# The spectrum's columns in two halves, input blocks contiguous over 128 lanes, and the tables and folds of the prologue in another order

## The chip, the cores and the metric

One core of a Trainium2 chip runs the kernel. The metric is the time of one execution on the device in microseconds (us), as a median over runs. The engines are TensorE (PE; its weight loads are PEld), VectorE (DVE), ScalarE (ACT) and GpSimd (POOL); SP (SyncE) issues nearly all DMA transfers, from one queue in program order, and waits there for whatever a transfer needs.

## The reference

```python
L = 2 * S                                   # x: (8, 6336, 128), h: (6336, 128)
Yf = np.fft.rfft(x, n=L, axis=1) * np.fft.rfft(h, n=L, axis=0)[None]
y = np.fft.irfft(Yf, n=L, axis=1)[:, :S, :]          # causal convolution along the sequence
scores = np.einsum('bsd,d->bs', y, w_gate)
# per batch: the 128 rows with the highest score
out[b, top] = y[b, top] + sigmoid(scores[b, top]) * (relu(y[b, top] @ w1) @ w2)
```

All arrays are float32. A long convolution of eight batches is followed by an expert that changes 128 rows of each batch.

## The kernel before

The transform is done by matmuls in four stages: with 6400 = 50 x 128, **a** transforms over 50 points, **b** over 128 points and multiplies by the spectrum of h, **c** and **d** go back. The work is cut into eight units (four pairs of batches times two halves of the 128 channels). A unit has eight input blocks of x.

- `load_x` loads a block (one transfer of SP); `place` says where it waits: in `half` (the tile into which c writes), in one of three tiles `xr`, or in the spectrum itself. `fold` makes sums and differences of the block, two operations on VectorE or POOL (L104, L105). A block has 114 lanes of data, of which 100 are used.
- `stage_a(unit, q, t)` transforms half of block q (L136) and copies the result from PSUM into the spectrum `reg[unit % 2]` (L146 on VectorE, L148 on ACT).
- `stage_b(unit, c)` takes four of the 50 columns k: matmuls with a table `wt` (L163), two products with the h spectrum `ht` on VectorE (L184), two additions on POOL into `reg` (L190). There are 13 per unit. `load_b` loads `wt` and `ht` for it.
- `stage_c(unit, a)` takes four of 64 columns j out of `reg` (L201) and copies them into `half` (L202). There are 16 per unit.
- `stage_d(unit, i)` makes the output (L218, then L221 to L223), POOL multiplies by the gate (L226, tile `tm`), VectorE reduces it (L230), and SP stores it. There are eight per unit; `load_d` loads its tables.
- The search for the highest scores and the experts run as a *strand* after every second unit: after each piece of other work `visit` issues a little of it.

`plan` writes the order out by hand. The prologue is a of h, a of unit 0, then "j" (b of h and b of unit 0 for the same columns, with the h spectrum stored to `hd` in between) and a of unit 1. Then for each unit u: c of u in pairs alternating with b of u+1 in pairs, and a of u+2 alternating with d of u. While c of u empties `reg[u % 2]`, blocks of unit u+2 are loaded into the columns that c has read; `AREAS` is the order in which c reads. b's tables come from six buffers and are asked for two b ahead. PSUM has three tiles `pt`, used in turn; the tiles that `wide` gives are five buffers.

The reads of `stage_c` and the place of a block in the spectrum are these lines:

```python
w = yv[:, r, c * 4 + j, :, t]               # yv: p (r j k t); c * 4 + j is one of 64 columns j
v4 = reg[u % 2].rearrange("p (c z) -> p c z", c=4)[0:LN, :, (q + 3) * 400:(q + 4) * 400]
return v4[:, :, 0:256], v4[:, :, 256:384]   # the block in four pieces, one in each quarter
```

## Time and profile before

| | |
|---|---|
| median of 3 runs | 1182.99 us (1181.5 to 1185.68) |
| profiled execution | 1172.5 us, span 1170.7 us |
| PE busy / PEld busy | 844.7 us (72%) / 743.8 us (64%) |
| DVE / POOL / ACT busy | 661.7 us (57%) / 555.7 us (47%) / 464.9 us (40%) |
| transfers | 147.03 MB, mean 126 GB/s; SP's queue takes 39.9% of the DMA engines' time |
| mean granted clock of TensorE | 0.870 |

Busy time is an average over stages with different limits, so the stages have to be looked at one by one. A granted clock of 1.00 is 2.4 GHz, 0.50 is 1.2 GHz.

### The profile page before, as it was taken

Reading aid. Unit: us, or ns where it says so; the run is one execution under the profiler, and the core shown is the slowest. Engines: PE = TensorE matmul, PEld = TensorE weight load, DVE = VectorE, ACT = ScalarE, POOL = GpSimd, SP = SyncE. Lnnn points to the kernel's source line nnn. Section 1 sums busy time; section 2 is a strip of 40 time slices with the busy share of each in tenths; the row PEclk is TensorE's granted clock in tenths of the full one; section 3 lists DMA queues with packets and bytes.
Section 4 is the critical chain, followed back from the end, with each engine's and each line's share of the span. In section 5 each row is a group of like instructions: output and inputs, shape, how many; then the busy total and the mean of one; then the engine's idle time right before and its main releaser. Section 6 shows DMA issues by size and latency. Waiting matters only on the chain. (4 is left out here: it accounts for less than half of the span.)

```text
span 1170.7 us, 36897 instructions
## 1 busy us (share of the span) xinstructions
PE 844.7 (72%) x16143; PEld 743.8 (64%) x16143; DVE 661.7 (57%) x1008; ACT 464.9 (40%) x1179; POOL 555.7 (47%) x392
## 2 busy tenths in 40 slices
PE   6849787786778687785778686785678998677303
PEld 5737676675667566774667565774677877676303
DVE  2228544453544567675585456575574786516773
ACT  3413331251125433762344333663343365572241
POOL 3427735653645545544555545344554565304402
PEclk9669898997889989997899988998898998888756
DMA  4345344355434643354335444355425443503300
GB/s 154 159 166 189 112 138 108 114 187 152 115 104 129 184 134 118 107 172 143 107 115 157 137 114 125 98 160 159 122 85 163 147 124 116 173 2 118 105 0 10
DMA packets 87149, 147.03 MB, mean 126 GB/s; under 512 B 6866, under 2 KB 42264, under 8 KB 86988
## 3 DMA queue, kind: packets, MB, share of 16 engines
q1 hardware_dynamic: 85964, 143.62, 39.9%
q8 instruction: 127, 2.08, 0.8%
q0 software_dynamic: 1024, 1.05, 0.4%
q14 instruction: 34, 0.28, 0.1%
HBM read 111.35 MB, written 33.29 MB: 124 GB/s over the span
## 5 line engine op out<-in xcount | busy, mean ns | idle before, releaser
L190 POOL TENSOR_TENSOR reg<-reg,tx 128x512 f32<-128x512 f32 (+1 forms) x208 | 265.4, 1304 | 289.3 <-DVE tx L184 224.7
L201 PEld LDWEIGHTS pt<-wc,reg 128*50 128x50 f32 x8192 | 272.2, 140 | 124.2 <-issue 60.0
L201 PE MATMUL pt<-wc,reg 128*50 128x64 f32 x8192 | 284.3, 236 | 86.2 <-DMA reg<-in_x 83.7
L202 ACT COPY half<-pt 114x1024 f32<-114x1024 f32 x128 | 141.9, 1109 | 386.8 <-PE pt L201 386.7
L163 PE MATMUL pt<-reg,wt 128*128 128x256 f32 x900 | 237.9, 417 | 73.2 <-DMA wt<-tab_wb 51.0
L163 PEld LDWEIGHTS pt<-reg,wt 128*128 128x128 f32 x900 | 174.5, 201 | 118.4 <-issue 74.2
L226 POOL TENSOR_TENSOR tm<-st,wg 114x1024 f32<-114x1024 f32 x64 | 151.9, 2374 | 200.3 <-DVE st L223 159.9
L184 DVE TENSOR_TENSOR reg<-pt,ht 128x1024 f32<-128x1024 f32 (+1 forms) x91 | 107.2, 1179 | 207.0 <-PE pt L163 165.6
L218 PE MATMUL pt<-half,at 114*50 114x128 f32 x2048 | 141.6, 294 | 37.2 <-ACT reg L148 29.0
L218 PEld LDWEIGHTS pt<-half,at 114*50 114x50 f32 x2048 | 125.8, 134 | 54.2 <-ACT reg L148 35.0
L148 ACT COPY reg<-pt 128x400 f32<-128x400 f32 x264 | 119.5, 540 | 63.7 <-PE pt L136 47.4
L308 ACT ACTIVATE junk<-key,nth 114x64 bf16<-114x64 f32 x332 | 115.6, 348 | 40.8 <-DVE nth L295 31.4
L222 DVE TENSOR_TENSOR st<-pt,st 114x512 f32<-114x512 f32 x64 | 44.2, 691 | 120.4 <-ACT st L221 120.1
L184 DVE TENSOR_TENSOR tx<-pt,ht 128x1024 f32<-128x1024 f32 (+1 forms) x91 | 106.6, 1172 | 0.0
L230 DVE TENSOR_REDUCE ss<-tm 114x16 f32<-114x1024 f32 x64 | 77.8, 1215 | 14.1 <-POOL tm L226 14.1
L221 ACT COPY st<-pt 114x512 f32<-114x512 f32 x64 | 37.7, 589 | 102.8 <-PE pt L218 54.2
L308 ACT ACTIVATION_READ_ACCUMULATOR junk<-key,nth 114x1 bf16 x332 | 63.0, 190 | 0.0
L287 PE MATMUL pm<-num,ones 114*114 114x6 bf16 (+1 forms) x59 | 10.4, 177 | 67.0 <-ACT junk L308 66.2
L136 PE MATMUL pt<-fa,reg 50*64 50x100 f32 x1920 | 49.9, 254 | 1.4 <-ACT reg L148 1.4
L136 PEld LDWEIGHTS pt<-fa,reg 50*64 50x64 f32 x1920 | 44.0, 136 | 7.0 <-issue 6.3
L223 DVE TENSOR_TENSOR st<-st,pt 114x512 f32<-114x512 f32 x64 | 44.0, 687 | 2.2
L136 PE MATMUL pt<-fa,xr 50*64 50x100 f32 x1408 | 38.0, 255 | 4.3 <-POOL xr L105 1.9
(99 smaller groups left out, 714.7 us busy)
## 6 DMA issues: line engine op xcount, KB each, us to landing
out<-st SPq DMA_DIRECT2D x128, 200.0 KB
wt<-tab_wb SPq DMA_DIRECT2D x96, 256.0 KB
at<-tab_at SPq DMA_DIRECT2D x128, 178.1 KB
ht<-hd SPq DMA_DIRECT2D x84, 256.0 KB
reg<-in_x SPq DMA_DIRECT2D x30, 456.0 KB
xr<-in_x SPq DMA_DIRECT2D x22, 456.0 KB
hd<-st SPq DMA_DIRECT2D x24, 256.0 KB
half<-in_x SPq DMA_DIRECT2D x12, 456.0 KB
```

The source lines that it names most:

```text
L136: nc.tensor.matmul(pt[c * 64:c * 64 + 64, b * 512 + j * 100:b * 512 + j * 100 + 100], w, tab[lanes, c], start=True, stop=True)
L148: nc.scalar.copy(out=dst, in_=src)
L163: nc.tensor.matmul(pt[:, k * 256:k * 256 + 256], wt[:, k], rows_of(unit, k0 + k), start=True, stop=True)
L184: v.tensor_tensor(out=dst, in0=pt[:, 0:n].rearrange("p (k b j t) -> p k b j t", b=4, j=32, t=2), in1=w, op=ALU.mult)
L190: g.tensor_tensor(out=y, in0=y, in1=tv[:, :, 1 - r], op=ALU.add if r else ALU.subtract)
L201: nc.tensor.matmul(pt[i * 64:i * 64 + N1, o:o + HD], w, wc[:, i], start=True, stop=True)
L202: nc.scalar.copy(out=hv[:, c * 4:c * 4 + 4].rearrange("p j r m t -> p (j r) t m"), in_=pt[0:LN].rearrange("p (j t m) -> p j t m", t=2, m=HD))
L218: nc.tensor.matmul(pt[a * 64:a * 64 + N1, r * 512 + c * 128:r * 512 + c * 128 + 128], ats[c // 2][0:LN, c % 2, a, r], hv[:, :, r, m], star ...
L222: v.tensor_tensor(out=st[:, 0:512], in0=pt[0:LN, 512:1024], in1=st[:, 512:1024], op=ALU.add)
L226: g.tensor_tensor(out=tm.rearrange("p (a d) -> p a d", d=HD), in0=st.rearrange("p (a d) -> p a d", d=HD), in1=wg[0:LN, u * HD:u * HD + HD] ...
L230: v.tensor_reduce(out=ss[u][:, :, :, 4 * i:4 * i + 4].rearrange("p b s c -> p s c b"), in_=tm.rearrange("p (s c b d) -> p s c b d", s=2, c ...
L308: nc.scalar.activation(out=junk, in_=cur[:, b], func=AF.Sign, bias=nth[:, b, j:j + 1], scale=-1.0, accum_out=num[:, b, j:j + 1])
```

## The change

The spectrum gets another order of columns: two halves h of 6400 columns, and within a half the real and imaginary part r, the batch b and 16 columns j. c reads one half first (`HALVES`), and four blocks of unit u+2 then lie in that half, each contiguous. The other four go to the `xr` tiles; there are three, so block 7 is loaded after a of block 4 has been done, and folded on POOL in front of a of block 6. Blocks, `fa` and the tables of d have 128 lanes (zeros in those that are not used) instead of 114. In the prologue blocks 16 to 23 are loaded during j instead of during a, the folds move with them, and a's copies are shared between ACT and VectorE for both halves of a block. The h spectrum is stored by planes (real and imaginary part apart). In j, VectorE's two operations that took PSUM and a tile from ACT become a third ACT operation and one VectorE operation on two tiles in SBUF:

```python
def stage_h(c, wt):
    ...
    turned, st = wide("turned")[:, 0:n], wide("st")[:, 0:n]
    ...
    straight = wide("straight")[:, 0:n]
    nc.scalar.mul(out=straight, in_=pt, mul=cst[:, 2:3])
    v.tensor_tensor(out=st.rearrange("p (a k d) -> p k a d", a=4, d=HD),
                    in0=straight.rearrange("p (k a d) -> p k a d", a=4, d=HD),
                    in1=turned.rearrange("p (k a d) -> p k a d", a=4, d=HD), op=ALU.add)
```

In `stage_b` VectorE's second product is written to `tx` in the order of the spectrum, so that POOL's additions run over eight contiguous elements instead of two. The rest of the diff, cut to its core:

```diff
-    hd = dp.tile([2, 128, N1, 2, HD], F32, name="hd")
+    hd = dp.tile([2, 128, 2 * N1 * HD], F32, name="hd")
...
     def view(r):
-        return reg[r].rearrange("p (r j k t) -> p r j k t", r=2, j=HD, t=2)
+        return reg[r].rearrange("p (h r b j k t) -> p h r b j k t", h=2, r=2, b=2, j=16, t=2)
...
     def place(n):
         u, q = n // 8 - 1, n % 8
-        if u >= 2 and q < 5:
-            v4 = reg[u % 2].rearrange("p (c z) -> p c z", c=4)[0:LN, :, (q + 3) * 400:(q + 4) * 400]
-            return v4[:, :, 0:256], v4[:, :, 256:384]
-        i = q + 5 if u >= 2 else n % 13
-        t = half[:, i * 1536:i * 1536 + 1536] if i < 10 else xr[i - 10]
-        return (t[:, 0:1024].rearrange("p (c z) -> p c z", c=4), t[:, 1024:1536].rearrange("p (c z) -> p c z", c=4))
+        if u >= 2 and q < 4:
+            o = 6400 + 1600 * (0, 2, 1, 3)[q]
+            return reg[u % 2][:, o:o + 1536]
+        i = 10 + (q - 4) % 3 if u >= 2 else n % 13
+        return half[:, i * 1536:i * 1536 + 1536] if i < 10 else xr[i - 10]
 
     def load_x(n):
         u, q = n // 8 - 1, n % 8
-        xs, es = place(n)
-        src = h[q] if u < 0 else x[u, q]
-        nc.sync.dma_start(out=xs, in_=src.rearrange("p (c z) -> p c z", c=4))
-        blocks[n] = (xs.rearrange("p c (d s m) -> p c d s m", d=2, s=2), es.rearrange("p c (d m) -> p c d m", d=2))
+        t = place(n)
+        nc.sync.dma_start(out=t[:, 0:1024], in_=h[q] if u < 0 else x[u, q])
+        blocks[n] = (t[:, 0:1024].rearrange("p (d s m) -> p d s m", d=8, s=2),
+                     t[:, 1024:1536].rearrange("p (d m) -> p d m", d=8))
 
     def fold(n, eng):
         xs, es = blocks[n]
-        eng.tensor_tensor(out=es, in0=xs[:, :, :, 0], in1=xs[:, :, :, 1], op=ALU.add)
-        eng.tensor_tensor(out=xs[:, :, :, 0], in0=xs[:, :, :, 0], in1=xs[:, :, :, 1], op=ALU.subtract)
+        eng.tensor_tensor(out=es, in0=xs[:, :, 0], in1=xs[:, :, 1], op=ALU.add)
+        eng.tensor_tensor(out=xs[:, :, 0], in0=xs[:, :, 0], in1=xs[:, :, 1], op=ALU.subtract)
...
-        ht = tp.tile([128, KC, 2, HD], F32, tag="w", name="ht", bufs=6)
-        nc.sync.dma_start(out=ht[:, 0:kn], in_=hd[unit % 2, :, k0:k0 + kn])
+        ht = tp.tile([128, 2 * KC * HD], F32, tag="w", name="ht", bufs=6)[:, 0:kn * 128]
+        nc.sync.dma_start(out=ht, in_=hd[unit % 2, :, k0 * 128:(k0 + kn) * 128])
...
-            nc.sync.dma_start(out=t[0:LN], in_=at_d[:, i, 2 * c:2 * c + 2])
+            nc.sync.dma_start(out=t, in_=at_d[:, i, 2 * c:2 * c + 2])
...
-                dst = view(unit % 2)[:, :, b * 32 + q * 4:b * 32 + q * 4 + 4, :, t]
+                dst = view(unit % 2)[:, q // 4, :, b, q % 4 * 4:q % 4 * 4 + 4, :, t]
...
-    AREAS = (3, 4, 5, 6, 7, 0, 1, 2)
+    HALVES = (4, 6, 12, 14, 0, 2, 8, 10)
...
-        return [[("c", unit, a), ("c", unit, a + 8)] for a in AREAS]
+        return [[("c", unit, a), ("c", unit, a + 1)] for a in HALVES]
...
-            fold(done[0], v if done[0] < 16 and done[0] % 3 == 0 else g)
+            fold(done[0], v if done[0] > 19 or done[0] < 16 and done[0] % 3 == 0 else g)
...
-                fold_to(n + q + 2)
-            stage_a(*s[1:], eng="both" if unit < 2 and t else None)
-            if t and unit < 2 and n + q + 13 < 24:
+                fold_to(min(n + q + 2, n + 7 if unit == 0 else 99))
+            if unit >= 2 and (q, t) == (6, 0):
+                fold(n + 7, g)
+            stage_a(*s[1:], eng="both" if unit < 2 else None)
+            if t and unit < 0 and q < 3:
                 load_x(n + q + 13)
-            if unit == 0 and q == 7 and t:
+            if unit >= 2 and (q, t) == (4, 1):
+                load_x(n + 7)
+            if unit == 0 and q == 0 and t:
                 load_constants()
             if t:
                 visit()
         elif kind == "j":
             stage_j(s[2], tabs.pop(s))
-            if s[2] >= 2:
-                fold_to(14 + s[2])
+            if s[2] < 8:
+                load_x(16 + s[2])
+            if s[2] in (3, 6, 9, 12):
+                fold_to(15 + s[2] // 3)
         elif kind == "b":
...
-            if unit + 2 < NU and s[2] >= 8:
-                i = AREAS.index(s[2] - 8)
+            if unit + 2 < NU and s[2] % 2:
+                i = HALVES.index(s[2] - 1)
                 m = (unit + 3) * 8
-                if i == 0:
-                    for q in range(5, 8):
-                        load_x(m + q)
-                elif i <= 5:
-                    load_x(m + i - 1)
+                for q in {0: (4, 5, 6), 2: (0, 1), 4: (2, 3)}.get(i, ()):
+                    load_x(m + q)
                 if i:
-                    fold(m + (4 + i if i < 4 else i - 4), v if i in (2, 4, 6) else g)
-                if i == 7:
-                    fold(m + 4, v)
+                    fold(m + (3 + i if i < 4 else i - 4), v if i in (2, 4, 6) else g)
             visit()
...
-        return z[..., 0:LN, :, :, :].reshape(a.shape[:-5] + (LN, 1024))
+        return z.reshape(a.shape[:-5] + (128, 1024))
```

In a stage where c of unit 0 alternates with b of unit 1, TensorE has these rows at the third c pair and behind it, with what each waits for. (`DMAHW` and a number is a transfer's semaphore, `pt` a PSUM tile; 32 rows of c are one `stage_c`, four of b one `stage_b`.) Before:

```order
L201 MATMUL pt_73<-wc,reg_74 50x64 [waits DMAHW1_49,Activation_49]
L201 MATMUL pt_73<-wc,reg_74 50x64 x31
L201 MATMUL pt_71<-wc,reg_74 50x64 [waits DVE_49]
L201 MATMUL pt_71<-wc,reg_74 50x64 x31
L163 MATMUL pt_72<-reg_75,wt 128x256 [waits DMAHW2_49,DVE_49]
L163 MATMUL pt_72<-reg_75,wt 128x256 x3
L163 MATMUL pt_73<-reg_75,wt 128x256 [waits DMAHW4_49,Activation_49]
L163 MATMUL pt_73<-reg_75,wt 128x256 x3
L201 MATMUL pt_71<-wc,reg_74 50x64 [waits DMAHW6_49,Activation_49]
```

After the change:

```order
L209 MATMUL pt_73<-wc,reg_74 50x64 [waits Activation_49]
L209 MATMUL pt_73<-wc,reg_74 50x64 x31
L209 MATMUL pt_71<-wc,reg_74 50x64 [waits DVE_49]
L209 MATMUL pt_71<-wc,reg_74 50x64 x31
L160 MATMUL pt_72<-reg_75,wt 128x256 [waits DMAHW1_49,DVE_49]
L160 MATMUL pt_72<-reg_75,wt 128x256 x3
L160 MATMUL pt_73<-reg_75,wt 128x256 [waits DMAHW3_49,Activation_49]
L160 MATMUL pt_73<-reg_75,wt 128x256 x3
L209 MATMUL pt_71<-wc,reg_74 50x64 [waits Activation_49]
```

c no longer waits for a transfer; it did at five of the eight pairs of the stage, and does at none now. b still waits for its table.

SP's queue in the same stage, from the three `xr` blocks on. Before:

```order
L99 DMA xr_76<-in_x 114x1024
L99 DMA xr_77<-in_x 114x1024
L99 DMA xr_78<-in_x 114x1024
L110 DMA wt<-tab_wb 128x512
L114 DMA ht<-hd 128x512
L110 DMA wt<-tab_wb 128x512
L114 DMA ht<-hd 128x512
L99 DMA reg_74<-in_x 114x4x256
L110 DMA wt<-tab_wb 128x512
L114 DMA ht<-hd 128x512
L110 DMA wt<-tab_wb 128x512
L114 DMA ht<-hd 128x512
```

After the change:

```order
L97 DMA xr_76<-in_x 128x1024
L97 DMA xr_77<-in_x 128x1024
L97 DMA xr_78<-in_x 128x1024
L109 DMA wt<-tab_wb 128x512
L113 DMA ht<-hd 128x512
L109 DMA wt<-tab_wb 128x512
L113 DMA ht<-hd 128x512
L109 DMA wt<-tab_wb 128x512
L113 DMA ht<-hd 128x512
L109 DMA wt<-tab_wb 128x512
L113 DMA ht<-hd 128x512
L97 DMA reg_74<-in_x 128x1024 x2
```

A block went out behind each c pair; now two go out together, behind the third and the fifth pair.

POOL, from the end of this stage (additions of b, L190 before and L197 after, and folds) through the eight `tm` products of d (L226 before and L234 after). Before:

```order
L190 TENSOR_TENSOR reg_75<-reg_75,tx 128x4x64x2 x4
L190 TENSOR_TENSOR reg_75<-reg_75,tx 128x2x64x2 x2
L104 TENSOR_TENSOR reg_74<-reg_74 114x4x128
L105 TENSOR_TENSOR reg_74<-reg_74 114x4x2x64
L226 TENSOR_TENSOR tm<-st,wg 114x1024 x8
```

After the change:

```order
L197 TENSOR_TENSOR reg_75<-reg_75,tx 128x2x32x8 x4
L197 TENSOR_TENSOR reg_75<-reg_75,tx 128x2x32x4 x2
L103 TENSOR_TENSOR reg_74<-reg_74 128x512
L104 TENSOR_TENSOR reg_74<-reg_74 128x8x64
L234 TENSOR_TENSOR tm<-st,wg 114x1024 x6
L103 TENSOR_TENSOR xr_76<-xr_76 128x512
L104 TENSOR_TENSOR xr_76<-xr_76 128x8x64
L234 TENSOR_TENSOR tm<-st,wg 114x1024 x2
```

The fold of block 7 now stands behind the sixth `tm` product, in the stage in which a of the same block is due.

## Rows read from the trace of the kernel before

**Rows 1.** Chain of waits, whole span: engine line, releaser, us in total, times, longest.
```profile
PE pt L201 <- DMA reg<-in_x: 83.7, 27, 4.6
...
PE pt L163 <- DMA wt<-tab_wb: 51.0, 6, 11.4
```

**Rows 2.** The same view for SP's DMA queue.
```profile
SPq L99 <- PE pt L201: 197.4, 30, 10.4
```

**Rows 3.** Windows, c/b stages: length; busy PE, PEld, DVE, ACT, POOL; clock; DMA share, GB/s.
```profile
150.90:229.80 78.90, 60.76 (x1125) 53.43 (x1124) 39.14 (x35) 17.19 (x16) 42.38 (x32) 0.91 0.46 132
...
388.60:474.80 86.20, 62.75 (x1135) 54.60 (x1130) 56.26 (x73) 31.93 (x88) 45.16 (x35) 0.88 0.45 129
...
917.30:978.50 61.20, 57.73 (x1147) 50.32 (x1147) 47.38 (x66) 34.84 (x92) 39.39 (x31) 1.00 0.42 122
sum 579.10, PE 435.05 PEld 379.87 DVE 346.45 ACT 198.15 POOL 303.98; mean PE 62.15 PEld 54.27 DVE 49.49 ACT 28.31 POOL 43.43
```

**Rows 4.** Timeline, 292 to 318 us: start, length, instructions, idle before them and releaser.
```profile
296.32 0.78 SPq L99 DMA_DIRECT2D reg<-in_x  x1
...
296.34 3.92 PE L163 MATMUL pt<-reg,wt 128*128 128x256 f32 x16
...
304.24 6.06 PE L201 MATMUL pt<-wc,reg 128*50 128x64 f32 x128 [3.98 <-DMA reg<-in_x]
...
310.23 3.91 PE L163 MATMUL pt<-reg,wt 128*128 128x256 f32 x16
```

**Rows 5.** Timeline of PE, 917 to 950 us.
```profile
926.95 3.79 PE L201 MATMUL pt<-wc,reg 128*50 128x64 f32 x128
930.96 3.92 PE L163 MATMUL pt<-reg,wt 128*128 128x256 f32 x16 [0.22 <-DVE tx L184]
```

**Rows 6.** Timeline, 262 to 292 us.
```profile
267.31 2.26 SPq L99 DMA_DIRECT2D xr<-in_x  x3
...
269.67 0.45 SPq L110 DMA_DIRECT2D wt<-tab_wb  x1
...
270.82 3.79 PE L201 MATMUL pt<-wc,reg 128*50 128x64 f32 x128
...
285.98 6.23 PE L163 MATMUL pt<-reg,wt 128*128 128x256 f32 x14 [11.37 <-DMA wt<-tab_wb]
```

**Rows 7.** Windows over the prologue.
```profile
0.00:60.20 60.20, 43.31 (x1024) 38.43 (x1024) 16.65 (x28) 23.52 (x48) 27.53 (x26) 0.77 0.40 157
60.20:132.80 72.60, 50.55 (x203) 38.19 (x201) 44.79 (x51) 16.54 (x27) 44.55 (x37) 0.88 0.50 175
```

**Rows 8.** Timeline, 0 to 40 us.
```profile
12.63 1.27 POOL L104 TENSOR_TENSOR half<-half 114x512 f32<-114x512 f32 x1 [0.36 <-DMA half<-in_h]
...
18.58 1.29 POOL L104 TENSOR_TENSOR half<-half 114x512 f32<-114x512 f32 x1 [3.34 <-DMA half<-in_h]
```

**Rows 9.** Groups of instructions by shape: busy us, mean ns of one; idle before and releasers.
```profile
L190 POOL TENSOR_TENSOR reg<-reg,tx 128x512 f32<-128x512 f32 x192 | 252.3, 1342 | 270.1 <-DVE tx L184 212.1 <-DVE ge L289 44.4 <-DVE nth L295 6.1
...
L184 DVE TENSOR_TENSOR tx<-pt,ht 128x1024 f32<-128x1024 f32 x84 | 101.9, 1213 | 0.0
...
L105 DVE TENSOR_TENSOR reg<-reg 114x512 f32<-114x512 f32 x18 | 23.9, 1330 | 0.6
...
L104 POOL TENSOR_TENSOR half<-half 114x512 f32<-114x512 f32 x15 | 19.1, 1273 | 28.2 <-DMA half<-in_h 17.0 <-DMA half<-in_x 9.4 <-PE pt L136 1.8
...
L173 DVE SCALAR_TENSOR_TENSOR st<-pt,cst,tm 128x512 f32<-128x512 f32 x24 | 16.9, 746 | 7.5 <-POOL reg L190 6.0 <-ACT tm L171 1.4
...
L171 ACT ACTIVATE tm<-pt,cst 128x512 f32<-128x512 f32 x24 | 15.2, 684 | 50.0 <-PE pt L163 39.6 <-DVE st L173 10.4
...
L104 DVE TENSOR_TENSOR half<-half 114x512 f32<-114x512 f32 x5 | 3.5, 692 | 21.7 <-DMA half<-in_h 12.6 <-DMA half<-in_x 9.0
```

**Rows 10.** Timeline, 246 to 264 us.
```profile
257.35 2.39 POOL L226 TENSOR_TENSOR tm<-st,wg 114x1024 f32<-114x1024 f32 x1 [1.80 <-DVE st L223]
...
259.20 1.60 PE L136 MATMUL pt<-fa,xr 50*64 50x100 f32 x64
```

87 lines of the change are left out of this document (43 added, 44 removed).

## The prediction

> **What bounds the kernel now.** I read the chain of waits first, then cut the span into its stages with the windows, then followed one stage in the timeline. Across the span TensorE waits 83.7 us in front of the c matmuls (L201) for loads of x blocks that c does not read, and 51.0 us in front of the b matmuls (L163) for their table [rows 1]. SP's queue stands 197.4 us at the x loads, waiting for c [rows 2]: load, c and load again hold each other up in turn.
>
> The stages show where. There are seven stages in which c of unit u alternates with b of unit u+1 ("c/b stages" below). Units 0 to 5 also load the eight x blocks of unit u+2 there; unit 6 has no such blocks left. The seven take 579.1 us, unit 6 alone 61.2, so the six with loads take 517.9, about 86 each [rows 3]. The work is the same: TensorE is busy 57.7 us in unit 6's stage and 60.8 in unit 0's, but there at a granted clock of 0.91 instead of 1.00. Unit 6 is thus a picture of a c/b stage without x loads, with a search strand running beside it.
>
> In unit 1's stage one round (a pair of c, a pair of b) starts at 296.34 with b; c begins only at 304.24, after 3.98 us on the DMA and at a slow pace (6.06 us); the next b starts at 310.23: 13.9 us [rows 4]. Unit 6 does a pair of c in 3.79 and a pair of b in 3.92 [rows 5], 7.7 us a round. The stage also has a hole near its start: three x blocks go out at 267.31, the table of the third b at 269.67 behind them, and that b starts at 285.98 instead of 274.6, where the second c pair ends [rows 6]. The DMA engines are not full meanwhile: their mean share is 0.45 and 0.46 in the stages shown [rows 3].
>
> **The change, part by part.**
>
> *Spectrum in halves, c by halves, x blocks contiguous.* The order of TensorE has a wait on a DMA in front of five of the eight c pairs of a stage before, and none after; SP issues the four blocks that lie in the spectrum in two pairs, each at least one c pair after the half is free. So the 3.98 us kind of wait goes, and with it SP's. A stage then costs TensorE 8 x 3.79 + 6 x 3.92 + 1.0 = 54.8 us [rows 5]. VectorE does 25 x 1.21 = 30 us of products [rows 9] and three folds of 1.4 to 2.7 us (now four): it has room in units 0 and 1 (39.1 busy before [rows 3]), less in units 2 to 5, where the search brings it to 56.3 in unit 2. I add 2 us for the third b's table and 3 us for folds that come in front of VectorE's products: 60 us for units 0 and 1. For units 2 to 5 I start from unit 6's 61.2 and add the same: 66. Together 120 + 264 = 384, against 517.9: **-134 us**. Bounds: 58 and 62 (nothing added but a little), 364; and 72 in all six, 432, if VectorE's 50 to 56 us must fit between TensorE's pieces.
>
> *All loads over 128 lanes.* Bytes grow by 12% (114 to 128 lanes). At the start, where only loads are waited for, POOL's folds of blocks 2 and 4 start at 12.63 and 18.58, both on the DMA [rows 8]: 2.98 us for each 0.467 MB block, 157 GB/s, with a DMA share of only 0.40 [rows 7]. So a queue full of loads leaves more than half of the engines idle. The price of a block of 0.524 MB lies between 3.3 us (the same 157 GB/s) and, if all engines take part at the b stage's 175 GB/s for a share of 0.50 [rows 7], 350 GB/s or 1.5 us. I take 1.8, near the low end, since tables over 128 lanes reach that ratio.
> The Trainium skill, "DMA: Bandwidth & Descriptors", section "Why a DMA increments its semaphore by 16 and not by 1", says a transfer uses the largest number of engines up to 16 that divides its slowest dimension: 114 gives 6, 128 gives 16. The share of 0.40 agrees (6 of 16 is 0.375). By that rule a block would take 2.98 x 6/16 x 128/114 = 1.25 us, an estimate from that page, and my 2 us at the third b would vanish, -12 us in all.
>
> *Prologue, a of h and of unit 0* (60.2 us [rows 7]). Sixteen blocks at 2.98 fill 48 of them. After: loads 16 x 1.8 = 29; POOL still folds ten of sixteen at 2 x 1.27 [rows 9], 25.5; TensorE is busy 43.3, at a clock of 0.77 [rows 7]. If that stays slow it sets about 7 + 40. I take 45 (35 with a full clock, 60 if nothing moves): **-15**. Blocks 16 to 23 now load later, during b of h, instead of in front of the tables.
>
> *Prologue, b of h with b of unit 0 ("j")* (72.6 us, of which VectorE is busy 44.8 [rows 7]). VectorE did two products off PSUM, 2 x 0.746, and two for unit 0, 2 x 1.21, per step [rows 9]: 3.9. Now one addition of 1024 columns with both operands in SBUF replaces the first two. No row has it; the nearest is the fold with 512 columns: 0.692 with POOL at rest, 1.330 beside POOL's work [rows 9], so 1.4 to 2.7; I take 1.9, since POOL is busy 61% of this stage. That is 4.3 a step, 12.5 steps, 54, and 6 to start and drain: 60 us, **-13** (51 to 72). The ACT copy added ("straight") is about twice 0.684 [rows 9] and lies beside: ACT then has 2.7 of every 4.3 us. A tile more per step in five buffers means that the second product of a step waits until the h spectrum of the step before has been stored; 5.0 us after its addition, it should be.
> The Trainium skill, "SBUF — State Buffer", section "Who interferes with whom", says that a VectorE operation with two SBUF inputs and a GpSimd one exclude each other for the whole instruction. This speaks against the edit; the pair 0.692 and 1.330 agrees. By it the addition could wait for one POOL piece (1.3) each step, 64 us rather than 60.
>
> *Units' a/d stages* (a of u+2 with d of u). Block 7 no longer has a place in the c/b stage: it loads after a(4) into the buffer of block 4, and POOL folds it behind six tm products. In unit 0's stage the sixth tm runs 257.35 to 259.74; the fold then ends 2 x 1.27 later, 262.3, but a(7) started at 259.20 [rows 10]. TensorE stalls **3.1 us**. Four such stages, and 2 us each in the two where the experts already stop TensorE: **+16** (6 to 25, if the load is late too). Behind a(7) stand d(7) and the next stage's c.
>
> *At nothing:* POOL's additions in runs of eight instead of two (its folds in runs of 64 take 1.273 for the same 512 elements, against 1.342 [rows 9], so at most 14 us of POOL time, hidden behind TensorE); h by planes (the same 2 KB per lane); a(0)'s and a(1)'s copies shared evenly between ACT and VectorE, and four folds of a(1) on VectorE: ACT loses what VectorE gains, and I leave a(1) as it is.
>
> **Sum.** The profiled execution took 1172.5 us (span 1170.7); the median shown is 1182.99, 1.009 times that. 1172.5 - 134 - 15 - 13 + 16 = 1026.5; times 1.009: **1036 us**.
>
> **Rivals.**
> 1. *VectorE takes over in the c/b stages.* For: 56.3 us busy in unit 2's stage, with search steps and folds in its one queue ahead of products that free PSUM. Against: unit 6 ran a search, VectorE 47.4 busy, in 61.2. All six at 72: 1172.5 - 86 - 12 = 1074.5, **1084**.
> 2. *Everything runs at TensorE's pace.* c/b 364 (-154), a of h and unit 0 35 (-25), j 52 (-20), a/d +6: 979.5, **988**. For: the clock of 1.00 in unit 6, where TensorE does not pause. Against: VectorE's and POOL's queues above.
> 3. *Bytes, not engines, bound the loads (slower).* Then a c/b stage still has to move its 10.4 MB (132 GB/s x 78.9 us) at the rate of these stages [rows 3]: no gain there, while the a/d stalls stay: 1172.5 + 16 = 1188.5, **1199**. It decides when the rate is capped near 124 GB/s: 6 x 10.4 MB then needs 502 us, and the gain is no more than the 16 lost. Against: j moved 175 GB/s [rows 7].
> 4. *The change doesn't do what it says*: the wait of c reappears as a wait of b for tables queued behind x pairs, and the time stays, **1183**. The first b of a c/b stage after the change has no fewer bytes ahead of it; but tables are asked for two b ahead, a full round of 7.7 us or more.
>
> **Numbers.** Forecast 0.50 (own range 1010 to 1065), rival 1 0.22, rival 2 0.20, rival 3 0.05, rival 4 0.03. The range 990 to 1095 leaves out rivals 3 and 4, half of what lies around rival 2's 988, and the top of rival 1. A measurement of this kernel tells about 0.3% from no change: faster 0.92 (the first three), same 0.03, slower 0.05.
>
> **What would show it.** The chain of waits without "PE L209 waits for reg<-in_x"; c/b stages of 58 to 68 us at a clock near 1.0; the third b of a stage at most 3 us late; a(7) about 3 us behind POOL's fold in each a/d stage; the first c at about 123 us instead of 150.9; the new addition at 1.4 to 2.7 us. I am wrong if c/b stages stay above 75 us, with b waiting for tables or c for VectorE, or if a(7) waits for its load.

## The result and the profile after

The changed kernel takes 1029.85 us (median of 4 runs, 1029.31 to 1032.79), the kernel before 1182.24 us on the same chip (1177.5 to 1185.68): a ratio of 0.8718, 95% interval 0.8683 to 0.8754. The forecast was 1036 us in a range of 990 to 1095. The profiled execution took 1030.3 us, its span is 1028.4.

The page of the changed kernel, its beginning and the 40 slices:

```profile
PE 804.8 (78%) x16143; PEld 707.2 (69%) x16143; DVE 676.9 (66%) x1015; ACT 472.2 (46%) x1168; POOL 566.7 (55%) x396
...
PEclk9999899999999999999888999999779998898556
...
GB/s 354 36 286 213 56 238 162 173 227 221 116 211 220 153 93 201 224 166 97 134 129 218 157 92 185 202 206 76 162 122 91 137 112 197 51 38 149 76 0 11
DMA packets 81736, 154.04 MB, mean 150 GB/s; under 512 B 8886, under 2 KB 32424, under 8 KB 81576
```

The first slice (25.7 us) moves 354 GB/s; the kernel before moved 154 in its first slice (29.3 us). The chain of waits (engine, line, releaser; us in total, times, longest) has no line "PE L209 waits for reg<-in_x" any more, which was 83.7 us [rows 1]. What there is:

```profile
ACT turned L172 <- POOL reg L197: 32.2, 11, 4.8
...
DVE st L175 <- ACT straight L174: 18.5, 8, 3.2
...
PE pt L135 <- POOL xr L103: 16.9, 6, 6.7
...
PE pt L135 <- POOL xr L104: 5.6, 6, 1.0
...
PE pt L160 <- DMA wt<-tab_wb: 3.5, 2, 1.9
```

The wait of b for its table, 51.0 us in [rows 1], is 3.5. The waits of a (L135) for GpSimd's folds in `xr` (L103 and L104) have grown from 1.9 us to 22.5, and those of ScalarE for GpSimd in j (L172, L171 before) from 2.9 to 32.2. The windows by stage (columns as in [rows 3]): the prologue in three rows, then the c/b stages of units 0, 1 and 2, and the a/d stages of units 0, 3 and 5:

```profile
0.00:44.43 44.43, 30.61 (x1024) 28.25 (x1024) 29.80 (x45) 17.82 (x32) 27.63 (x24) 0.96 0.60 221
44.43:107.58 63.15, 50.42 (x204) 37.65 (x201) 44.63 (x38) 27.95 (x38) 42.26 (x29) 0.97 0.62 216
107.58:127.27 19.69, 14.93 (x512) 13.53 (x512) 15.24 (x25) 9.03 (x18) 6.42 (x6) 0.83 0.11 40
127.27:181.21 53.94, 53.94 (x1129) 47.34 (x1125) 37.90 (x34) 17.42 (x16) 41.79 (x33) 1.00 0.61 195
181.21:216.34 35.13, 28.20 (x772) 25.40 (x770) 16.44 (x20) 19.47 (x40) 21.48 (x11) 1.00 0.61 188
216.34:272.14 55.80, 53.93 (x1128) 47.29 (x1125) 40.37 (x36) 17.66 (x16) 44.19 (x34) 1.00 0.61 196
...
310.11:373.68 63.57, 55.30 (x1133) 47.94 (x1129) 52.92 (x71) 32.23 (x88) 43.59 (x33) 1.00 0.53 170
...
480.73:541.46 60.73, 48.49 (x846) 42.19 (x842) 29.58 (x56) 22.77 (x49) 28.60 (x19) 0.83 0.45 133
...
712.16:776.54 64.38, 46.77 (x832) 40.87 (x829) 26.66 (x52) 22.30 (x48) 25.23 (x16) 0.79 0.40 122
```

In unit 0's c/b stage TensorE is busy 53.94 of 53.94 us at a granted clock of 1.00 (2.4 GHz): there is nothing left there to wait for. The gain is in these stages and at the start; j gained less than it could, and the a/d stages became longer.

For all kernels of this study the stages are cut in the same way: TensorE's first b ends "a of h and a(0)", its first c ends the prologue, and each first c and first a in turn bounds the c/b and a/d stages of units 0 to 5. The sums over six stages, in us, of the profiled executions (the rest, from c of unit 6 on, is 251.9 to 256.3 in every one of them):

| kernel | a of h, a(0) | j | a(1) | six c/b | six a/d | ratio to before |
|---|---|---|---|---|---|---|
| before | 60.2 | 72.6 | 18.1 | 518.1 | 248.3 | 1 |
| changed | 44.4 | 63.2 | 19.7 | 367.1 | 282.2 | 0.8718 (0.8683 to 0.8754) |
| changed, 114 lanes | 66.6 | 64.9 | 20.1 | 424.3 | 283.7 | 0.9593 (0.954 to 0.9646) |
| before, 128 lanes | 46.9 | 53.8 | 17.3 | 369.5 | 245.1 | 0.8535 (0.8478 to 0.8592) |
| before, 112 + 2 lanes | 53.1 | 55.3 | 16.8 | 388.7 | 250.6 | 0.8689 (0.8648 to 0.8729) |
| before, 128 lanes, blocks only | 48.5 | 53.7 | 17.7 | 370.6 | 254.0 | 0.8587 (0.8534 to 0.8639) |
| before, 128 lanes, copies added | 47.2 | 53.8 | 17.5 | 375.4 | 252.8 | 0.8586 (0.8545 to 0.8627) |
| before, 128 lanes, loaded twice | 48.9 | 53.8 | 17.3 | 479.4 | 241.5 | 0.9548 (0.9496 to 0.96) |
| changed, early fold | 44.0 | 63.3 | 20.1 | 372.4 | 240.5 | 0.8555 (0.8515 to 0.8596) |
| changed, j's buffers apart | 44.9 | 56.9 | 18.0 | 367.3 | 275.2 | 0.8782 (0.8711 to 0.8853) |
| changed, both | 45.0 | 55.4 | 18.8 | 368.9 | 255.8 | 0.8494 (0.845 to 0.8537) |
| changed, early fold, j's old form | 44.1 | 50.3 | 18.0 | 372.9 | 248.2 | 0.845 (0.8417 to 0.8482) |
| changed, again | 45.7 | 63.2 | 20.1 | 366.3 | 274.7 | 0.8798 (0.8758 to 0.8838) |

The runs stood beside the kernel before on their own chip, where it took 1159.66 to 1169.91 us. The changed kernel's own ratio is 0.8718 on one chip and 0.8798 on another, so a difference of less than 1% between kernels on different chips is read from stage lengths, not from ratios.

### The profile page after: what moved, and what is told of

Its sections match the earlier page's. It is cut to its first block, busy times and chain, and to the rows that moved or that the text cites. A ratio compares the mean times of both kernels' runs of the same rounds, so it can differ in the third digit from the quotient of the medians.

```text
span 1028.4 us, 36824 instructions
## 1 busy us (share of the span) xinstructions
PE 804.8 (78%) x16143; PEld 707.2 (69%) x16143; DVE 676.9 (66%) x1015; ACT 472.2 (46%) x1168; POOL 566.7 (55%) x396
## 5 line engine op out<-in xcount | busy, mean ns | idle before, releaser
L197 POOL TENSOR_TENSOR reg<-reg,tx 128x512 f32<-128x512 f32 (+1 forms) x208 | 269.8, 1325 | 148.9 <-DVE tx L191 123.6
L234 POOL TENSOR_TENSOR tm<-st,wg 114x1024 f32<-114x1024 f32 x64 | 152.0, 2375 | 216.8 <-DVE st L231 160.2
L209 PEld LDWEIGHTS pt<-wc,reg 128*50 128x50 f32 x8192 | 241.1, 129 | 40.9 <-issue 35.4
L209 PE MATMUL pt<-wc,reg 128*50 128x64 f32 x8192 | 251.6, 223 | 1.1 <-DVE bb L290 1.1
L160 PE MATMUL pt<-reg,wt 128*128 128x256 f32 x900 | 224.5, 399 | 31.6 <-DVE tx L191 27.0
L210 ACT COPY half<-pt 114x1024 f32<-114x1024 f32 x128 | 143.1, 1118 | 228.5 <-PE pt L209 224.8
L160 PEld LDWEIGHTS pt<-reg,wt 128*128 128x128 f32 x900 | 164.4, 189 | 73.9 <-DVE tx L191 31.6
L226 PE MATMUL pt<-half,at 114*50 114x128 f32 x2048 | 149.4, 303 | 30.1 <-ACT reg L147 24.1
L226 PEld LDWEIGHTS pt<-half,at 114*50 114x50 f32 x2048 | 132.1, 139 | 51.4 <-ACT reg L147 29.0
L147 ACT COPY reg<-pt 128x400 f32<-128x400 f32 x240 | 112.0, 542 | 77.1 <-PE pt L135 65.6
L316 ACT ACTIVATE junk<-key,nth 114x64 bf16<-114x64 f32 x332 | 115.7, 349 | 47.3 <-DVE nth L303 37.9
L135 PE MATMUL pt<-fa,xr 50*64 50x100 f32 x1792 | 53.6, 267 | 23.5 <-POOL xr L103 16.9
L135 PEld LDWEIGHTS pt<-fa,xr 50*64 50x64 f32 x1792 | 46.1, 145 | 30.3 <-POOL xr L103 18.3
L135 PE MATMUL pt<-fa,reg 50*64 50x100 f32 x1536 | 45.6, 265 | 4.1 <-issue 3.2
L303 DVE SCALAR_TENSOR_TENSOR nth<-cst,bb 114x6 f32<-114x6 f32 (+1 forms) x59 | 43.5, 737 | 5.8 <-DVE bb L300 0.9
```

Source lines behind the costliest of these rows:

```text
L135: nc.tensor.matmul(pt[c * 64:c * 64 + 64, b * 512 + j * 100:b * 512 + j * 100 + 100], w, tab[lanes, c], start=True, stop=True)
L147: nc.scalar.copy(out=dst, in_=src)
L160: nc.tensor.matmul(pt[:, k * 256:k * 256 + 256], wt[:, k], rows_of(unit, k0 + k), start=True, stop=True)
L197: g.tensor_tensor(out=yv[:, :, r], in0=yv[:, :, r], in1=zv[:, :, 1 - r], op=ALU.add if r else ALU.subtract)
L209: nc.tensor.matmul(pt[i2 * 64:i2 * 64 + N1, o:o + HD], w, wc[:, i2], start=True, stop=True)
L210: nc.scalar.copy(out=hv[0:LN, c * 4:c * 4 + 4].rearrange("p j r m t -> p (j r) t m"), in_=pt[0:LN].rearrange("p (j t m) -> p j t m", t=2, ...
```

## The experiments

My theory was the prediction's: the new order of the spectrum takes the wait for blocks out of c, and the lanes only shorten loads. The rival to test first was that the lanes do it all. The first two kernels have one half of the change each; the next two try the two places where the changed kernel lost time.

**The changed kernel over 114 lanes.**

```python
-        nc.sync.dma_start(out=t[:, 0:1024], in_=h[q] if u < 0 else x[u, q])
+        t = t[0:LN]
+        nc.sync.dma_start(out=t[:, 0:1024], in_=(h[q] if u < 0 else x[u, q])[0:LN])
...
-            nc.sync.dma_start(out=t, in_=at_d[:, i, 2 * c:2 * c + 2])
+            nc.sync.dma_start(out=t[0:LN], in_=at_d[0:LN, i, 2 * c:2 * c + 2])
```

> The changed kernel, with the blocks, the a tables and the d tables loaded over 114 lanes again; the contiguous places, the order of the loads and all the rest stay. My theory: the place alone takes TensorE's wait for the blocks out of c, so c shows no wait for in_x here either; the lanes are worth something in two other places. A block would again take about 2.98 us as in [rows 8], so the third b of the stages would again wait for its tables, by up to the 51.0 us of [rows 1] where the changed kernel shows 3.5, and the a's of h and the first unit would end at 60 us again where they now end at 44.4. Sum: 1030 + up to 47 + 15 = about 1070 to 1092 us. Rival 1, the lanes do nearly all (short loads are why c does not wait): c/b stages near their old 518 us and 1150 to 1183 us. Rival 2, the lanes do nothing that is not hidden: 1030 to 1035 us.

Measured: 1116.05 us against 1159.66, ratio 0.9593. c does not wait for blocks, as the theory said. The time is above my 1092: the start took 66.6 us, where I had 60, and the wait for tables came back larger than I allowed, with 51.0 us in [rows 1]:

```profile
PE pt L161 <- DMA wt<-tab_wb: 67.8, 13, 11.8
```

TensorE's timeline in unit 1's stage (c is L210 and b L161 here):

```profile
255.18 3.78 PE L210 MATMUL pt<-wc,reg 128*50 128x64 f32 x128
270.74 5.71 PE L161 MATMUL pt<-reg,wt 128*128 128x256 f32 x16 [11.78 <-DMA wt<-tab_wb]
276.38 3.79 PE L210 MATMUL pt<-wc,reg 128*50 128x64 f32 x128
```

The hole of [rows 6] is still there, 11.78 us instead of 11.37; the rounds behind it run without a stop. The change without the lanes, the place above all, is worth 93.8 us in the six c/b stages and 4.1% of the whole.

**The kernel before over 128 lanes.**

```python
-    xr = [cp.tile([LN, 1536], F32, name="xr%d" % i) for i in range(3)]
-    half = cp.tile([LN, 2 * 128 * HD], F32, name="half")
+    xr = [cp.tile([128, 1536], F32, name="xr%d" % i) for i in range(3)]
+    half = cp.tile([128, 2 * 128 * HD], F32, name="half")
...
-            v4 = reg[u % 2].rearrange("p (c z) -> p c z", c=4)[0:LN, :, (q + 3) * 400:(q + 4) * 400]
+            v4 = reg[u % 2].rearrange("p (c z) -> p c z", c=4)[:, :, (q + 3) * 400:(q + 4) * 400]
...
-            nc.sync.dma_start(out=t[0:LN], in_=at_d[:, i, 2 * c:2 * c + 2])
+            nc.sync.dma_start(out=t, in_=at_d[:, i, 2 * c:2 * c + 2])
```

> The kernel before, with one part of the change: blocks, a tables and d tables are loaded over 128 lanes. The four pieces a block is split into in the spectrum's columns, the order of loads and the h spectrum stay. My theory: a wait of c lasts as long as a block's transfer, so 27 waits of 3.1 us on average [rows 1] shrink with the transfer but do not go: 83.7 us to about 40. The third b's 51.0 us shrink to under 15, the start gains about 15. Sum: 1183 - 43 - 36 - 15 = about 1089 us, 1070 to 1120. Rival 1, the place is all: c waits for 80 us still, and only the start gains: about 1165 us. Rival 2, the lanes are all: 1030 to 1045 us, with the contiguous place worth nothing.

Measured: 988.97 us, ratio 0.8535: better than the whole change, and beyond what even the rival gave it. The blocks still lie in four pieces among the columns, and c no longer waits for them; two lines of the chain of waits:

```profile
PE pt L163 <- DMA wt<-tab_wb: 3.4, 2, 1.9
...
PE pt L201 <- DMA reg<-in_x: 2.3, 4, 0.9
```

83.7 us have become 2.3, not 40. A round of the same unit's stage as in [rows 4], from the timeline:

```profile
234.53 0.55 SPq L99 DMA_DIRECT2D reg<-in_x  x1
234.54 3.91 PE L163 MATMUL pt<-reg,wt 128*128 128x256 f32 x16
...
238.43 3.79 PE L201 MATMUL pt<-wc,reg 128*50 128x64 f32 x128
```

The load is issued when b begins, and c starts 3.90 us after the issue, with no idle time; in [rows 4] it started 7.92 us after it. So the wait is what is left of the landing after the pair of b. My theory falls: the place was not needed once the loads were quick. Ahead of the changed kernel it is in j and in the a/d stages; the windows of j and of the a/d stages of units 0 and 5:

```profile
46.87:100.65 53.78, 48.03 (x201) 36.60 (x201) 44.77 (x51) 16.80 (x28) 41.48 (x34) 1.00 0.51 177
...
172.16:206.19 34.03, 27.91 (x772) 25.29 (x770) 16.52 (x21) 19.29 (x40) 19.23 (x10) 1.00 0.57 170
...
686.34:732.52 46.18, 38.80 (x830) 34.68 (x827) 28.74 (x54) 20.96 (x46) 20.12 (x12) 0.93 0.51 153
```

**The fold of block 7 earlier.**

```python
-            if unit >= 2 and (q, t) == (6, 0):
+            if unit >= 2 and (q, t) == (5, 0):
                 fold(n + 7, g)
```

> The changed kernel, with the fold of block 7 written one block earlier in the program: ahead of a(5) instead of ahead of a(6), so that GpSimd does it one step (4.2 us) earlier. Its load is issued where it was. My theory: a(7) waits for its fold alone, which stands behind GpSimd's gate multiplication and, with the experts, behind their indirect transfers: TensorE shows 16.9 + 5.6 us of waits for L103 and L104 in the changed kernel, and most of it goes: 1030 - 18 = about 1012 us, 1007 to 1018. Rival 1: the block has not landed one step earlier, or the gate multiplication behind the fold is late and d waits in its place: 1026 to 1032 us. Rival 2: it goes in the stages without experts (2.7 to 4 us in each of four) and not in the two with them, where the chain of the experts sets the time: about 1018 to 1022 us.

Measured: 994.42 us, ratio 0.8555 (the changed kernel: 0.8718 and 0.8798). In unit 0's a/d stage the fold now lies one step earlier, and a(7) starts with no wait:

```profile
206.27 1.27 POOL L103 TENSOR_TENSOR xr<-xr 128x512 f32<-128x512 f32 x1
...
207.63 1.29 POOL L104 TENSOR_TENSOR xr<-xr 128x512 f32<-128x512 f32 x1
...
208.87 2.38 POOL L234 TENSOR_TENSOR tm<-st,wg 114x1024 f32<-114x1024 f32 x1
209.97 1.60 PE L135 MATMUL pt<-fa,xr 50*64 50x100 f32 x64
```

No wait of L135 for L103 or L104 on `xr` is left. Against the second run of the changed kernel (the last one below, 1020.99 us) the gain is 26.6 us; by the first ratio, 0.8718, it would be 19. There were 22.5 us of waits to remove. In the profiled executions the a/d stages shrink by 34.2 us and the c/b stages grow by 6.1, of which b's waits for tables account for 3.9 (8.3 against 4.4). Rival 2 left out the two stages with experts. The second of them takes 49.7 to 53.9 us in the three kernels with the early fold and 60.1 to 64.4 in the three executions over 128 lanes without it, so there the rival falls; in the first (47.5 to 57.7 against 55.2 to 60.7) the two overlap.

**j's two ScalarE tiles out of the five wide buffers.**

```python
-        turned, st = wide("turned")[:, 0:n], wide("st")[:, 0:n]
+        st = wide("st")[:, 0:n]
+        turned, straight = (half[:, o + c % 2 * 2048:o + c % 2 * 2048 + n] for o in (0, 1024))
...
-        straight = wide("straight")[:, 0:n]
```

> The changed kernel, with turned and straight of the j stage in the part of half that is free then (two places for each, in turn), so that only st and tx use the five wide buffers. My theory: in j the step takes 4.9 us, where TensorE's products take 3.95 and VectorE's three operations 3.7, because ScalarE's turned waits for the buffer that GpSimd's addition of the step before holds (32.2 us of such waits in 11 times); with the buffers apart a step takes 4.0 to 4.3 us, and j 53 to 57 us instead of 63.2: 1030 - 8 = 1020 to 1024 us. Rival 1, the three PSUM pairs bound the step (TensorE shows 1.9 us <- tx once per two steps): ScalarE's wait moves, j stays at 61 to 64 us, 1028 to 1031 us. Rival 2, the new addition on VectorE is what makes the step long: it stays too.

Measured: j 56.9 us instead of 63.2, inside the theory's 53 to 57; ScalarE no longer waits for GpSimd's addition there. The whole gave 1015.69 us with a ratio of 0.8782 (0.8711 to 0.8853), too wide to show 6 us.

**Both together, and j's old form.** The second kernel has the early fold and replaces j's addition from SBUF:

```python
-        straight = wide("straight")[:, 0:n]
-        nc.scalar.mul(out=straight, in_=pt, mul=cst[:, 2:3])
-        v.tensor_tensor(out=st.rearrange("p (a k d) -> p k a d", a=4, d=HD),
-                        in0=straight.rearrange("p (k a d) -> p k a d", a=4, d=HD),
-                        in1=turned.rearrange("p (k a d) -> p k a d", a=4, d=HD), op=ALU.add)
+        for a in range(4):
+            v.scalar_tensor_tensor(out=st.rearrange("p (a k d) -> p a k d", a=4, d=HD)[:, a],
+                                   in0=pt.rearrange("p (k a d) -> p a k d", a=4, d=HD)[:, a], scalar=cst[:, 2:3],
+                                   in1=turned.rearrange("p (k a d) -> p a k d", a=4, d=HD)[:, a],
+                                   op0=ALU.mult, op1=ALU.add)
```

> The changed kernel with both edits: the fold of block 7 one block earlier, and turned and straight of j in half. If the two are independent, as their places in the trace say (j ends at 107 us, the first a/d stage begins at 181), their gains add: the first alone stands at 0.8555 of the kernel before, the second takes j from 63.3 to 56.9 us, 6.4 us or 0.0055: ratio 0.850 (0.846 to 0.854). Rival: what j gains is given back in a of unit 1 and the first c/b stage: 0.8555 again.

> The changed kernel with the early fold, and with j's h spectrum formed as before: VectorE multiplies the products in PSUM by the scalar and adds turned (four operations, one for each plane), no straight copy on ScalarE and no addition from SBUF. The kernel before with 128 lanes shows j at 53.8 us, 3.7 to 3.8 us a step, with this form. My theory: the new form is the reason that j takes 63.2 us in the changed kernel, not the layout of the spectrum or the x loads put into j; j then takes 54 to 56 us and the ratio is 0.8555 - 9/1160 = 0.847 (0.843 to 0.851). Rival: the loads of blocks 16 to 23 and their folds on GpSimd, which the change moved into j, are what makes it long: j 60 to 63 us and a ratio of 0.853 to 0.857.

Measured: ratio 0.8494 for the first, 0.845 for the second. The first ratio is what the two gains add up to, and j is at 55.4 us; but the interval (0.845 to 0.8537) overlaps that of the early fold alone, and in the profiled execution the a/d stages took 255.8 us against 240.5, so that the gains add is not shown by the whole time. In the second, j takes 50.3 us, against 63.3 with the early fold alone and the same x loads and folds inside it, so the new form is what made j long, and the rival falls. The windows and VectorE's groups (count; busy us, mean ns; idle before) in j of this kernel:

```profile
44.09:94.35 50.26, 48.09 (x202) 36.58 (x201) 47.39 (x75) 16.57 (x27) 35.09 (x29) 1.00 0.77 274
```

```profile
L174 DVE SCALAR_TENSOR_TENSOR st<-pt,cst,turned 128x256 f32<-128x256 f32 x48 | 19.8, 475 | 2.7 <-ACT turned L172 2.6
```

Four operations of 475 ns, 1.9 us a step, are longer than the one addition of 1.3 us in the changed kernel, and j is 12.9 us shorter all the same. That is the lowest ratio measured here: its interval, 0.8417 to 0.8482, lies below the changed kernel's on either chip, but meets those of the kernel with both edits and of the kernel before with 128 lanes.

**Copies in front of the loads.** To see whether c depends on the landing at all over 128 lanes, I put more bytes ahead of it, in the kernel before with 128 lanes:

```python
+        if u >= 2 and q < 5:
+            nc.sync.dma_start(out=spare[(u - 2) * 5 + q], in_=src)
```

> The kernel before with 128 lanes, where c waits 2.3 us for in_x in all although the blocks are still in four pieces among the columns that c reads. Added: ahead of each load into the spectrum a copy of the same block from memory to memory (30 copies of 0.524 MB, on the same queue), which nobody waits for. My theory: c does wait for the landing of the load, but the pair of b between two pairs of c covers it: the load is issued at 234.53, b runs to 238.43, and 0.524 MB at 350 to 385 GB/s are landed shortly before. With 1.4 us or more of other bytes ahead of it the landing comes after b, and c waits again, 0.5 to 3 us each: 15 to 80 us of waits for in_x, 1000 to 1060 us. Rival: over 128 lanes c does not depend on the load at all; waits for in_x stay under 5 us, the bytes are hidden, 985 to 1000 us.

Measured: 6.2 us of waits in 9 times, longest 1.4, and 1002.9 us. This decides little. A copy waits for nothing and so was issued in front of SP's wait for c, about 3.4 us ahead of its load (234.50 and 237.92 in the timeline); the bytes were moved in an idle gap. It was a dose in the wrong place.

**Each such block loaded twice.** The second load has to wait for the first, so nothing can go ahead:

```python
-        nc.sync.dma_start(out=xs, in_=src.rearrange("p (c z) -> p c z", c=4))
+        for i in range(2 if u >= 2 and q < 5 else 1):
+            nc.sync.dma_start(out=xs, in_=src.rearrange("p (c z) -> p c z", c=4))
```

> The kernel before with 128 lanes; each block that goes into the spectrum's columns is loaded twice, one load after the other into the same place, the second issued when the first has landed. The copies of the run with double bytes went out early, in front of the wait for c, and so delayed little; here nothing can go ahead. My theory: c waits for the landing, and over 128 lanes the landing (about 3 to 3.5 us after the issue) is just covered by the b pair (3.9 us). With two in a row c waits 2.2 to 3.5 us in each of some 27 places: 60 to 95 us of waits for in_x, much as the 83.7 us of the kernel before [rows 1], and 1045 to 1085 us. Rival: over 128 lanes c does not depend on the load; waits under 5 us, 985 to 1000 us.

Measured: c (L202 here) waits again, and SP (L100) shows how long a first load is on its way:

```profile
PE pt L202 <- DMA reg<-in_x: 99.2, 29, 4.4
```

```profile
SPq L100 <- DMA reg<-in_x: 99.5, 30, 4.5
```

SP waits 99.5 / 30 = 3.3 us after issuing the first load until it has landed; with the issue of 0.5 us that is 3.8 to 3.9, just what a pair of b takes (3.92 in [rows 5]). The rival falls. The six c/b stages grow by 109.9 us, 97 of them these waits, and the time to 1105.56, above my 1085: the waits are a little longer than I gave, and TensorE's granted clock in these stages was 0.92 to 0.96, where it was 0.97 to 1.00. The tables behind the second load were not late: b waits 3.5 us for them, and 3.4 without the second load.

**What makes a load quick: 112 lanes and two.** The kernel before with each block and d table in two transfers, and no other edit:

```python
-        nc.sync.dma_start(out=xs, in_=src.rearrange("p (c z) -> p c z", c=4))
+        for o, e in ((0, 112), (112, LN)):
+            nc.sync.dma_start(out=xs[o:e], in_=src[o:e].rearrange("p (c z) -> p c z", c=4))
...
-            nc.sync.dma_start(out=t[0:LN], in_=at_d[:, i, 2 * c:2 * c + 2])
+            for o, e in ((0, 112), (112, LN)):
+                nc.sync.dma_start(out=t[o:e], in_=at_d[o:e, i, 2 * c:2 * c + 2])
```

> The kernel before, 114 lanes as before, with each x and h block and each d table loaded by two DMAs: 112 lanes and the last 2. Nothing else. My theory: what counts is on how many DMA engines a load is spread, and 112 lanes spread over as many as 128 do; then c's waits for in_x go from 83.7 us to under 10, and the time is near that of the kernel before with 128 lanes, 985 to 1010 us (twice as many DMAs stand in SP's queue, at 0.3 to 0.6 us each). Rival: the padding to 128 lanes itself counts (whole tiles without a gap): 1100 to 1160 us, c still waits.

Measured: 1016.98 us, ratio 0.8689, and c (L203 here) hardly waits:

```profile
PE pt L203 <- DMA reg<-in_x: 6.3, 13, 1.0
```

Same bytes, same tiles, same places: these two edits give what the whole change gave, so the padding is not what counts. The c/b stages are 19.2 us longer than with 128 lanes; b waits 10.8 us for its table there. The transfers of 1 to 13 us, busy share of the DMA engines in tenths and GB/s in slices of 0.3 us, of the kernel before, of the changed one and of this one:

```profile
DMA  0032442234333333433333333334333333333333
GB/s 0 0 37 69 123 121 76 96 109 164 164 150 137 164 164 164 164 150 164 164 164 150 150 164 164 150 137 164 164 164 150 164 164 164 164 150 150 164 150 150
```

```profile
DMA  0018927999999997998899998999999999999999
GB/s 0 0 29 248 283 82 246 382 396 410 437 355 410 382 273 246 300 300 328 369 396 341 341 355 355 410 423 423 396 382 410 423 410 437 423 437 437 423 437 423
```

```profile
DMA  0023989996779799899989989989988998999999
GB/s 0 0 37 75 289 323 358 328 300 164 205 232 287 273 246 232 232 287 300 232 191 259 191 205 300 273 164 273 232 178 246 287 205 218 259 191 218 273 232 205
```

With the queue full of blocks, a third of the engines was busy at 137 to 164 GB/s before; over 128 lanes nine tenths are, at 410 to 437 in the last ten slices. The trace also has a start and a length for each packet that was moved. Between 4 and 12 us six of them, at times seven, are in flight at once before; over 128 lanes, and with 112 + 2, the median is sixteen. A packet of 4 KB takes 159 ns both before and over 128 lanes, so the rate grows with the number in flight. With 112 + 2 a packet takes 273 ns, and the rate stays at 164 to 300 GB/s; why, no run shows.
The Trainium skill, "DMA: Bandwidth & Descriptors", section "Why a DMA increments its semaphore by 16 and not by 1", says that a transfer is spread over the largest number of engines, up to 16, that divides its slowest dimension; by it 114 lanes use 6, 112 and 128 use 16. The counts of six and sixteen in flight agree.

**Blocks alone over 128 lanes, tables over 114.**

> The kernel before with the blocks of x and h alone over 128 lanes; the d tables and the a tables over 114 as before. My theory: the blocks carry the gain, since a/d stages were no longer with 114 lanes than with 128 in the changed kernel (283.8 and 282 us over the six units): ratio 0.855 to 0.865 (the run with all over 128: 0.8535). Rival: the d tables, of which six are issued at the end of a c/b stage ahead of the next loads, hold a good part of it: 0.88 to 0.93.

Measured: 998.61 us, ratio 0.8587, with 370.6 us of c/b stages. The blocks carry the gain; the tables add 0.5%, which is no more than two chips differ by.

**The changed kernel again.**

> The changed kernel as it is, on the chip of these runs. Ratio 0.868 to 0.876 as before. The open point: its two a/d stages with experts took 60.7 and 64.4 us, with TensorE's a matmuls coming in short pieces during the gathers, where the runs with the early fold show 47.5 to 57.7 us. If these pieces belong to the kernel's order, they come again at 59 to 65 us; if they belong to an execution, one of the two stages is at 48 to 56 us here.

Measured: 0.8798, just above what I gave, and a/d stages of 55.2 and 60.1 us with experts. TensorE's waits of L135 for nothing that the trace shows are 1.9 us here, 8.9 in the first execution. Most of the short pieces of a during the gathers thus belong to one execution, though the second of these stages is as long as if they were the kernel's; the wait of a(7) for GpSimd is the kernel's, here 4.63 and 6.84 us in these two stages.

## Why the prediction was right, and where it was not

The time was right to 0.6%, but partly by luck: the largest term was given to the wrong part of the change, the term for j came from a wrong account of that stage, and two errors of 17 and 18 us cancel.

- **c/b stages, -134 us:** measured 518.1 - 367.1 = -151.0, inside the bounds. What failed is the step "The order of TensorE has a wait on a DMA in front of five of the eight c pairs of a stage before, and none after ... So the 3.98 us kind of wait goes". The order does take c's wait away, also over 114 lanes, but it was not needed: with the old order and 128 lanes the same stages take 369.5, the waits 2.3 us. I priced the wait by its length in [rows 4] and asked only whether the order keeps it. The sum to make was landing minus cover: 7.92 us from issue to c, 3.9 of them covered by b, so a landing shorter by 4 us removes the wait whole. The parts do not add: the change without the lanes gives -93.8, the lanes alone -148.6, both -151.0.
- **Why the landing fell by 4 us and not by the 1.2 us of "I take 1.8":** the 2.98 us were read at the start, and a block of the c/b stages took longer. By the packets of the trace, the block of [rows 4] goes in 456 packets of 1 KB, six to seven in flight at once, from 297.9 to 303.5 us: 5.6 us. A packet takes 46 ns at first, and 68 to 87 ns (medians of half a microsecond) from 300 us on, when packets of the tables issued behind it are in flight beside it. Over 128 lanes (the block issued at 234.53) 512 packets of 46 ns, sixteen to seventeen at once, take 2.0 us, and nearly all are through before the first packet of a table. Over 24 such blocks the mean is 5.9 us before and 2.3 with 128 lanes. At 46 ns throughout, 456 packets, six at a time, would take 3.5 us, an estimate; the slower packets make most of the rest.
- **Third b's table:** "2 us for the third b's table" per stage; 3.5 us in all. Without the lanes it would have been 67.8, so this, too, was the lanes.
- **Block load of 1.8 us:** at 410 to 437 GB/s 0.524 MB take 1.20 to 1.28 us. The rule of the Trainium skill, "DMA: Bandwidth & Descriptors", section "Why a DMA increments its semaphore by 16 and not by 1", gave an estimate of 1.25 in the prediction; the trace agrees, and I took the dearer value.
- **Start, -15 us:** measured -15.8. With the lanes alone it is -13.3; the rest of the change has the other 2.4 (1.2 in the second execution). Over 114 lanes the rest makes it 6.4 us longer; what does it is told under j.
- **j, -13 us:** measured -9.4, of the right sign for a wrong reason. By the prediction's own count the edit makes a step longer, 3.9 to 4.3 us, and the old form should have taken 12.5 x 3.9 + 6 = 55 us, where 72.6 were measured. The step that failed is to read j as VectorE's operations. Most of the missing 17 us were one hole, and no row of the prediction shows it: VectorE, ahead of its first operation on j's products, stood waiting for a constant table, and TensorE for VectorE.

```profile
80.55 0.23 DVE L520 CAST upper<-half 114x128 bf16<-114x128 f32 x1 [19.08 <-DMA half<-tab_tri]
...
82.30 8.02 PE L163 MATMUL pt<-reg,wt 128*128 128x256 f32 x24 [16.33 <-DVE st L173]
```

With 128 lanes and nothing else this wait is gone, and j is at 53.8 us, -18.8. The changed kernel also issues the constants earlier, in a of unit 0; over 114 lanes the hole moves there, and makes the start longer:

```profile
55.01 0.23 DVE L529 CAST upper<-half 114x128 bf16<-114x128 f32 x1 [14.50 <-DMA half<-tab_tri]
```

The new form then costs part of the gain. "I take 1.9" for the addition was too dear: it took 1.3 us on average, and 1.22 where it started ahead of GpSimd. So it waited for GpSimd about 0.1 us a step, not 1.3; the 64 us that the prediction gave for that wait (12.5 x 1.3 would be 16 us more, not 4) lie near the measured 63.2 by chance. What went wrong with it is "A tile more per step in five buffers means that the second product of a step waits until the h spectrum of the step before has been stored; 5.0 us after its addition, it should be". The wait came at another tile: `turned` takes the buffer that `tx` held, so ScalarE waits for GpSimd. The timeline of the changed kernel shows it, 4.78 us once in two steps of 4.9, and behind it VectorE waiting for `straight`:

```profile
75.75 1.26 ACT L172 ACTIVATE turned<-pt,cst 128x512 f32<-128x512 f32 x2 [4.78 <-POOL reg L197]
...
76.90 1.11 ACT L174 ACTIVATE straight<-pt,cst 128x1024 f32<-128x1024 f32 x1
78.12 1.41 DVE L175 TENSOR_TENSOR st<-straight,turned 128x1024 f32<-128x1024 f32 x1 [2.32 <-ACT straight L174]
```

With buffers of their own 6 to 8 us of j go; 5 to 7 more go with the old form, which leaves out a ScalarE pass between TensorE and VectorE. Of this second part the runs do not tell how much is that pass and how much GpSimd.
- **a/d stages, +16 us:** measured +33.9, and +26.4 in the second execution; the mechanism was right, the size was not. Unit 0's stall was 1.76 + 0.96 us where I had 3.1. In the stages with experts I gave 2 us, and GpSimd stood behind its own indirect transfers there. The fold ends of unit 5:

```profile
766.19 0.99 POOL L452 DMA_INDIRECT out<-xe,iu  x1 [3.83 <-DMA out<-xe,iu]
767.20 1.27 POOL L103 TENSOR_TENSOR xr<-xr 128x512 f32<-128x512 f32 x1
768.53 0.59 PE L135 MATMUL pt<-fa,xr 50*64 50x100 f32 x2 [6.72 <-POOL xr L103]
```

- **At nothing:** GpSimd's additions in runs of eight took 1374 ns, 1342 before [rows 9]: no gain, as taken. a(1) is 1.6 us longer.
- **Sum:** -15.8 - 9.4 + 1.6 - 151.0 + 33.9 = -140.7, and -1.5 in the rest: 1170.7 becomes 1028.4, to 0.1. The gain forecast 17 us too small and the loss forecast 18 us too small cancel. The factor "1.009 times that" did not hold either: the profiled execution took 1030.3 us and the median 1029.85, so the factor put 9 us too much on the forecast.
- **Rivals:** rival 3 (bytes bound the loads) falls with 195 GB/s in unit 0's c/b stage, rival 1 (VectorE takes over) with stages of 54 to 67 us, rival 4 (b waits for tables instead) with 3.5 us. Rival 2 was nearest for the c/b stages, 364. A rival was missing: that one part of the change, the lanes, does it all and the rest costs. On top of 128 lanes the rest of the change adds 43.8 us (1028.4 against 984.6 of span; 37.9 in the second execution; by the ratios 1.8 to 2.6% of the time before); with the fold one step earlier and j as before it adds 1.0 (985.6).

What stays open: why TensorE's a came in short pieces during the gathers of one execution of the changed kernel and less so in the other, and why a packet of 4 KB takes 273 ns with 112 + 2 lanes.

## What to carry to other kernels

Look at the DMA engines' busy share while a queue is full of one kind of load: here a share of a third with a long queue meant that six packets were in flight instead of sixteen, and cutting the transfer at a multiple of 16 lanes was a two-line test that could have come before any change of layout or order. A wait on a transfer is landing minus cover: before pricing an edit by the length of the wait, work out how much shorter the landing must be for the cover to hide it. Count the stage as it is with the same terms as the stage to come: where the count falls short of what was measured, as in j by 17 us, a wait is missing from the account, and it may be what the change removes. When a change has several parts, price each as if it were the only one, and ask of each further part what is left for it to save; here the largest part made the others a loss.
